# Seven products for ten instead of eight weight pairs in the second layer of a fused attention-plus-Mish block (Trainium2, one core)

## The chip, the cores and the metric

The kernel runs on one core of one Trainium2 chip. The metric is the device time of one execution in microseconds. An execution is timed as a whole; one more execution was profiled, and its record gives the start and the duration of every instruction on the engines: PE (TensorE, matmuls), PEld (its weight loads), DVE (VectorE), ACT (ScalarE), POOL (GpSimd) and SP (SyncE, which issues nearly all DMAs here). PSUM is the memory that PE writes and that DVE and ACT read.

## The reference

2048 tokens of 576 features, float32. One layer norm feeds two branches, and both are added to the input:

```python
xn = _layernorm(x)
q, k, v = split_heads(xn @ wqkv)            # 32 heads of 18
# each token attends to 8 tokens: itself and those 2, 4, ..., 14 before it
o = softmax_over_8(q . k * scale, mask) . v
A = o @ wo
h = xn @ w1 + b1                            # 4608 features (in reference: einsum)
B = (h * tanh(softplus(h))) @ w2            # Mish, then back to 576
return x + A + B
```

(The sketch keeps the arithmetic of the reference and shortens its code. In the reference the second branch is fed `xn`, too.)

## The kernel before, in words

**Precision.** Every matmul operand is kept as a high part (rounded to fp32r by an ACT cast) and a low part (the difference, taken by DVE or POOL). A product is three matmuls: high x high, high x low, low x high. So each weight tile and each activation costs a cast and a subtraction, on ACT and on DVE or POOL.

**Tiling.** The tokens are done in two halves (`hf` 0 and 1) of 1024, each in two blocks of 512 (`b`). The 4608 features of the hidden layer are 36 tiles of 128, taken as 18 pairs (`q`). In the second half the pairs come in the order 1, 2, ..., 17, 0 (`Q1`), but are still counted from 0.

**First layer** (`m1_part`, line 748). For one pair, 2 token blocks times 2 feature tiles are computed by seven products instead of eight, in six parts m0 to m5. PSUM banks are re-used inside a pair: `mish(hf, q, 1, 1, cur[3], cur["c22"])` at the end of m3 asks DVE (line 728) to add bank 3 and a copy `c22`, which ACT took from bank 1 at the end of m3 (line 717); m4 goes on accumulating in bank 3, so it must wait for this add. After the add come Mish (ACT, 729), the cast (ACT, 734) and the low part (POOL, 735).

**Second layer, the plain way** (`m2_pair` in the first half, `m2_cols` in the second, lines 783 and 896). A pair's activations times its two `w2` tiles: 4 chunks of 24 matmuls of 288 columns, with an eviction by DVE (lines 787, 899) for every six.

**Second layer by seven products** (second half only, for the first 2 x `OC` pairs, `p_item`, line 875). Two pairs together form a group `e`; token block x column half is a 2 x 2 scheme, done by seven items of 24 matmuls. It needs sums of weight quarters, T1 to T4, which the first half prepares when it meets a pair with 1 <= q <= 2 x `OC`: `t_sum` (line 304: T3 on DVE, T1, T2, T4 on POOL), `t_high` (ACT cast, 310), `t_low` (DVE, 315), `t_keep` (two DMAs to DRAM each). In the second half it needs sums of activations (`u_sum`, 817), casts (`u_high`, 823) and low parts (`u_low`, 829), and each item fetches its weights (`p_fetch`, 843). Pair q = 2 x `OC` of the second half is held raw and split by `a_split`.

**Attention.** The projections q, k, v (line 351, and `z_part`, 449, which does the last two groups of the second half by seven products with weight sums `z_...`) go to DRAM and come back as windows. A generator `attention(hf)` makes 73 steps for each half: eight head groups of nine steps. Of the nine, four multiply q by k (POOL, two instructions of line 542 each), one subtracts the maximum and calls the exponential, four multiply by v (POOL, two of line 580 each). The reduction of a product (DVE, 547 or 586) is held back and issued at the next step. After a group's last reduction, DVE transposes (606) and SP sends the result to DRAM (`o_send`, 615: four DMAs, eight for the last group).

**Output projection** (`wo_part`, line 1079): eight items of three parts at the end, by seven products too, on tiles `oa`, `ob`, `oS` that `o_split` makes (lines 927 to 958); their sources come by `o_load` (908), the sums of the first half by `y_load` (1054).

**The order of the work** is written out by hand. `plan` is a list of slots, each with one piece of PE work. A slot has a list `[1]` of things issued before its PE work (`before(i, fn)`) and a list `[0]` of its PE work and what is issued behind it. Inside a slot the order is: what the last slot left in `soon`, list `[1]` in the order in which it was filled, the Mish chains that the last slot left in `pend`, then list `[0]`. The engines keep this order:

```python
for fn in first + bg + (fns + held if i == at["m", 0, 1, 0] else held + fns):
```

For a pair of the first half, `spot(0, q, i)`, i = 0 to 9, are the slots m0, m1, chunk, m2, chunk, m3, chunk, m4, chunk, m5 (from q = 2 on); "slot 3 of pair 9" below means spot(0, 9, 3). Attention steps go to slots by a clock: every slot has a planned length, times a rate of its region (`marks`, `rate`), and a step falls due every 6.111 units, in the next allowed slot (in pairs from 1 on: slots 0, 3, 7 and 9). In the second half the slots of the steps are listed (`early`). `t_...` steps stand at slots 2 to 7 of a pair: T1 at 2, T2 at 3, T4 at 4, the cast of T3 and T1 at 4, the cast of T2 and T4 at 5. They are filled in ahead of the attention steps, so in one slot they come first.

## Time and profile before

| what | value |
|---|---|
| time, median of three | 1106.52 us (1106.3 to 1106.97) |
| time of the profiled execution | 1106.93 us |
| its span, first to last instruction | 1105.1 us |
| matmuls of `m2_pair` / `m2_cols` / `p_item` | 1728 / 960 / 672 |
| busy share: PE, DVE, ACT, POOL | 99%, 77%, 45%, 72% |

The 1.8 us between the span and the time lie around the program. A row of the timeline reads: start, duration, engine, line, operation, output tile <- input tiles, shape, count, and in brackets how long the engine stood idle before it and who ended that. Where several instructions are merged, the duration is that of all of them. A row of the windows reads: window, its length, then for PE, PEld, DVE, ACT and POOL the busy time and the number of instructions, the granted clock, the DMA share and GB/s.

### The profile page before, as it was taken

To read this page: it belongs to the slowest core of one execution; us is meant where nothing else is said; L and a number is where in the kernel's file an instruction comes from. 1 tells how busy PE (TensorE), PEld (TensorE's weight loads), DVE (VectorE), ACT (ScalarE), POOL (GpSimd) and SP (SyncE) were. 2 spreads that over 40 slices of the span, in tenths; PEclk is the share of its full clock that TensorE was granted. 3 is DMA by queue.
4 is the path that set the end of the run, shared out by engine and by line. 5 is a ranking of instruction groups with operands and counts; after the bars stand their busy time and mean duration, and the time that the engine had idled before them with its cause. 6 is when DMAs were issued, how large, how long until landed. Compare 5 with 4: busy or idle time off the path is not lost.

```text
span 1105.1 us, 18208 instructions
## 1 busy us (share of the span) xinstructions
PE 1098.0 (99%) x6550; PEld 1014.0 (92%) x6550; DVE 849.1 (77%) x1367; ACT 499.1 (45%) x917; POOL 790.8 (72%) x639
## 2 busy tenths in 40 slices
PE   8999999999999999999999999999999999999998
PEld 7999899999999999999999888989999999999998
DVE  6368788888889888888656567777886777777786
ACT  5544655544545543646333354434433344343353
POOL 2479777776769688685789568567698976867542
PEclk9999999999999999999999999999999999999999
DMA  6899696868777768676598799656674657776674
GB/s 200 286 311 313 231 335 244 283 234 263 254 269 242 272 225 293 234 265 219 171 316 277 237 348 327 228 192 209 222 225 171 211 196 224 244 293 216 181 232 140
DMA packets 178270, 271.60 MB, mean 246 GB/s; under 512 B 53218, under 2 KB 120068, under 8 KB 178180
## 3 DMA queue, kind: packets, MB, share of 16 engines
q1 hardware_dynamic: 178180, 270.44, 72.1%
q8 instruction: 52, 0.85, 0.3%
q14 instruction: 38, 0.31, 0.1%
HBM read 160.39 MB, written 110.00 MB: 245 GB/s over the span
## 4 chain that ended last, share of the span: by engine, by line
PE 92%; DMA 3%; DVE 2%; ACT 1%; SPq 1%; POOL 1%; issue 1%; DVEq 0%; POOLq 0%
PE h L683 28%; PE po L783 21%; PE po L896 11%; PE pq L351 11%; PE po L875 6%; PE h L689 5%; PE o L1079 5%; PE z L449 3%; DMA accP<-in_x 1%; DMA t<-kept_t 1%; DMA kv<-kv_d 1%; SPq L615 1%; DMA pw<-kept_T 0%; POOL act L735 0%; DMA acc<-in_x 0%
## 5 line engine op out<-in xcount | busy, mean ns | idle before, releaser
L783 PEld LDWEIGHTS po<-w,act 128*128 128x128 f32 x1728 | 236.3, 188 | 5.8 <-POOL act L735 0.4
L783 PE MATMUL po<-w,act 128*128 128x288 f32 x1728 | 240.6, 295 | 0.1
L542 POOL TENSOR_TENSOR pr<-q,kv 128x576 f32<-128x576 f32 x128 | 198.1, 1575 | 8.8 <-DMA q<-q_d 5.6
L735 POOL TENSOR_TENSOR act<-c,act 128x512 fp32r<-128x512 f32 x81 | 107.6, 1328 | 127.5 <-ACT act L734 126.1
L580 POOL TENSOR_TENSOR pv<-L,kv 128x576 f32<-128x576 f32 x128 | 177.9, 1488 | 26.1 <-DVE L L573 21.3
L787 DVE TENSOR_TENSOR acc<-po,acc 128x288 f32<-128x288 f32 x288 | 119.2, 448 | 29.2 <-PE po L783 28.3
L351 PE MATMUL pq<-wq,xt 128*128 128x432 f32 x672 | 136.2, 361 | 1.1 <-ACT xt L81 1.1
L896 PEld LDWEIGHTS po<-w,act 128*128 128x128 f32 x960 | 130.9, 188 | 2.8
L896 PE MATMUL po<-w,act 128*128 128x288 f32 x960 | 132.9, 295 | 0.0
L351 PEld LDWEIGHTS pq<-wq,xt 128*128 128x128 f32 x672 | 125.0, 188 | 7.8 <-ACT xt L81 1.6
L729 ACT ACTIVATE c<-c,b1c 128x512 f32<-128x512 f32 x81 | 58.7, 725 | 137.9 <-DVE c L728 137.6
L683 PE MATMUL h<-xt,t 128*128 128x512 f32 x432 | 110.5, 391 | 0.4 <-DVE rt L728 0.4
L683 PE MATMUL h<-S,t 128*128 128x512 f32 x432 | 110.4, 391 | 0.0
L586 DVE TENSOR_REDUCE og<-pv 128x144 f32<-128x1152 f32 x64 | 85.9, 1345 | 24.0 <-POOL pv L580 23.8
L683 PE MATMUL h<-xt,wa 128*128 128x512 f32 x432 | 103.9, 389 | 0.0
L717 ACT COPY c<-h 128x512 f32<-128x512 f32 x81 | 47.4, 585 | 123.1 <-PE h L689 72.0
L547 DVE TENSOR_REDUCE L<-pr 128x64 f32<-128x1152 f32 x64 | 85.8, 1342 | 21.8 <-POOL pr L542 21.7
L683 PEld LDWEIGHTS h<-xt,wa 128*128 128x128 f32 x432 | 81.0, 188 | 16.6
L875 PEld LDWEIGHTS po<-pw,u 128*128 128x128 f32 x672 | 91.9, 188 | 2.2
L875 PE MATMUL po<-pw,u 128*128 128x288 f32 x672 | 93.4, 294 | 0.0
L683 PEld LDWEIGHTS h<-xt,t 128*128 128x128 f32 x432 | 79.1, 188 | 15.3 <-DVE rt L728 0.9
L899 DVE TENSOR_TENSOR accP<-po,accP 128x288 f32<-128x288 f32 x160 | 68.9, 452 | 30.3 <-PE po L896 29.3
(228 smaller groups left out, 1851.4 us busy)
## 6 DMA issues: line engine op xcount, KB each, us to landing
kv<-kv_d SPq DMA_DIRECT2D x64, 396.0 KB, 5.0
kept_t<-t SPq DMA_DIRECT2D x36, 512.0 KB, 4.9
t<-kept_t SPq DMA_DIRECT2D x36, 512.0 KB, 6.6
rw<-in_w SPq DMA_DIRECT2D x36, 320.0 KB, 4.4
kept_wa<-wa SPq DMA_DIRECT2D x18, 640.0 KB, 4.6
kept_w<-w SPq DMA_DIRECT2D x20, 576.0 KB, 4.0
wa<-kept_wa SPq DMA_DIRECT2D x18, 640.0 KB, 5.3
w<-kept_w SPq DMA_DIRECT2D x20, 576.0 KB, 4.3
```

The source lines that it names most:

```text
L351: nc.tensor.matmul(pq[:, 0:432], XT[:, xi, tok], wt[wi][:, hl, 0:432], start=i == 0, stop=i == len(seq) - 1)
L542: nc.gpsimd.tensor_tensor(out=pr[:, x:x + hh], in0=q[:, j0 + x:j0 + x + hh, None, :].to_broadcast([P, hh, W, CU]), in1=win(kt, 0, CU, j0 + ...
L547: nc.vector.tensor_reduce(L[:, k, j0:j0 + hj].rearrange("p j w h -> p (j w h)"), pr.rearrange("p j w (h d) -> p (j w h) d", h=2), axis=AX, ...
L580: nc.gpsimd.tensor_tensor(out=pr[:, x:x + hj].rearrange("p j d w -> p j w d"), in0=L[:, k, x:x + hj, :, h:h + 1].to_broadcast([P, hj, W, DH]),
L586: nc.vector.tensor_reduce(og[:, c0:c0 + DH, :].rearrange("p d j -> p j d"), pr, axis=AX, op=ALU.add)
L683: nc.tensor.matmul(ph, wt[:, wl, wk * P:(wk + 1) * P], X[:, xs, :], start=first and i == 0, stop=last and i == len(seq) - 1, skip_group_ch ...
L735: nc.gpsimd.tensor_tensor(out=a[:, 1, :], in0=t, in1=a[:, 0, :].bitcast(F32), op=ALU.subtract)
L783: nc.tensor.matmul(po, acts[hf, q, b, j][:, al, tok], done["w2", hf, 2 * q + j][:, wl, c * HC:(c + 1) * HC], start=i == 0, stop=i == 5)
L787: nc.vector.tensor_tensor(out=t, in0=po, in1=t, op=ALU.add)
L875: nc.tensor.matmul(po, units[e, k, qq][:, al, tok], w[:, qq, wl, :], start=i == 0, stop=i == 5)
L896: nc.tensor.matmul(po, acts[hf, q, b, j][:, al, tok], done["w2", hf, 2 * q + j][:, wl, c * HC:(c + 1) * HC], start=i == 0, stop=i == 5)
L899: nc.vector.tensor_tensor(out=t, in0=po, in1=t, op=ALU.add)
```

## The change

`OC` goes from 4 to 5: five groups instead of four, so ten pairs of the second half are done by seven products. Everything that hangs on `OC` follows: pairs 9 and 10 of the first half now make T1 to T4, and pairs 8 and 9 of the second half (counted from 0) lose their `m2_cols` and are held raw for group 4. With it:

- Pair 10's block (1, 0) rests in slot `r3`.
- For q over 8, `t_low` stands behind the slot's PE work (list `[0]`). So do all the low parts of the `z` weights. The `z` weight work starts at slot 6 of pair 10, not slot 4 of pair 9, with both its rounds 28 slots apart.
- First half's attention: the rate from pair 16 on is 1.05 (it was 0.8), and one step instead of three lies in the second half's first pair. The steps up to pair 16 keep their slots.
- Second half's attention: `early` has three steps in pair 0 (it had one), one more in pair 5 and a longer list. Its last step lies one slot later, in the third instead of the second of the last four chunks.
- The preparation of `wo` starts at slot 0 of pair 13, not slot 3 of pair 11, with tighter spacing.

```diff
-OC = 4
+OC = 5
@@ raw_act
-...[b, j][q % {(1, 0): 4, (1, 1): 2}.get((b, j), 3)]
+...[b, j][3 if (q, b, j) == (2 * OC, 1, 0) else q % {(1, 0): 4, (1, 1): 2}.get((b, j), 3)]
@@ t steps of a pair
-            before(i + d, lambda f=f, name=name, q=q: f(q, name))
+            plan[i + d][f is not t_low or q <= 8].append(lambda f=f, name=name, q=q: f(q, name))
@@ z weights
-    i = spot(0, 9, 4)
+    i = spot(0, 10, 6)
-                d = 30 + 2 * n + (n >= 14) if k else 2 * n if n < 10 else (19, 20, 22, 23, 25, 26, 27)[n - 10]
-                before(i + d, lambda f=f, name=name, k=k: f(name, k))
+                d = 28 * k + (2 * n if n < 10 else (19, 20, 22, 23, 25, 26, 27)[n - 10])
+                plan[i + d][kind != "o"].append(lambda f=f, name=name, k=k: f(name, k))
@@ attention steps
-    behind_next.add(at["m", 1, 10, 3])
+    behind_next.add(at["m", 1, 2 * OC + 2, 3])
-    marks = [..., spot(0, 1, 0), spot(0, 2 * OC + 1, 0), at["q", 1, 0, 0, 0],
+    marks = [..., spot(0, 1, 0), spot(0, 9, 0), spot(0, 16, 0), at["q", 1, 0, 0, 0],
-    rate = (1.15, 0.4, 0.5, 0.8, 1.15, 1.25, 0)
+    rate = (1.15, 0.4, 0.5, 0.8, 1.05, 1.15, 1.25, 0)
-    last_steps = [spot(1, 0, i) for i in (0, 2, 4)]
+    last_steps = [spot(1, 0, 0)]
-    early = {0: (8,), 1: (0, 2, 4, 6, 8), 2: (0, 4, 7), 3: (0, 3, 6), 4: (0, 4, 7), 5: (0, 3, 7), 6: (1, 4, 7),
-             7: (0, 4, 7), 8: (1, 4, 8), 9: (1, 3, 7)}
+    early = {0: (2, 4, 8), 1: (0, 2, 4, 6, 8), 2: (0, 4, 7), 3: (0, 3, 6), 4: (0, 4, 7), 5: (0, 3, 6, 8),
+             6: (1, 4, 7), 7: (0, 3, 7), 8: (1, 4, 7), 9: (0, 4, 7), 10: (1, 4, 8), 11: (1, 3, 7)}
@@ wo weights
-    i = spot(1, *(11,3))
+    i = spot(1, 13, 0)
-        k = i + 10 + (2, 5, 10, 15, 20, 25, 30, 35, 40)[n]
+        k = i + 10 + (2, 5, 8, 12, 15, 19, 23, 27, 31)[n]
```

More of the change, by code (lines that the diff above doesn't have):

```diff
@@ L703, in raw_act @@
         tag, n = {(0, 0): (("raw", 0), ("raw", 1), ("raw", 2)), (1, 0): (("mn", 2), ("mn", 3), ("mn", 0), ("r3", 0)),
-                  (0, 1): (("raw", 3), ("mn", 4), ("mn", 1)), (1, 1): (("tt", 0), ("tt", 1))}[b, j][q % {(1, 0): 4, (1, 1): 2}.get((b, j), 3)]
+                  (0, 1): (("raw", 3), ("mn", 4), ("mn", 1)), (1, 1): (("tt", 0), ("tt", 1))}[b, j][3 if (q, b, j) == (2 * OC, 1, 0) else q % {(1, 0): 4, (1, 1): 2}.get((b, j), 3)]
         if (tag, n) not in rslot:
@@ L1507, in block_kernel @@
             ok[spot(0, q, i)] = i in (0, 3, 7, 9) and (q > 1 or i)
-    marks = [at["q", 0, 2, 0, 1], at["q", 0, 3, 0, 0], spot(0, 1, 0), spot(0, 2 * OC + 1, 0), at["q", 1, 0, 0, 0],
+    marks = [at["q", 0, 2, 0, 1], at["q", 0, 3, 0, 0], spot(0, 1, 0), spot(0, 9, 0), spot(0, 16, 0), at["q", 1, 0, 0, 0],
              at["z", 0, 0], spot(1, 0, 0)]
-    rate = (1.15, 0.4, 0.5, 0.8, 1.15, 1.25, 0)
+    rate = (1.15, 0.4, 0.5, 0.8, 1.05, 1.15, 1.25, 0)
     T = [0.0]
```

## The prediction

> **What bounds the kernel now.** I read the page first, then the chain of waits, then the timeline engine by engine around the places that the diff touches.

> ```profile
> PE 1098.0 (99%) x6550; PEld 1014.0 (92%) x6550; DVE 849.1 (77%) x1367; ACT 499.1 (45%) x917; POOL 790.8 (72%) x639
> PEclk9999999999999999999999999999999999999999
> PE 92%; DMA 3%; DVE 2%; ACT 1%; SPq 1%; POOL 1%; issue 1%; DVEq 0%; POOLq 0%
> ```

> PE is busy nearly all the time at a high granted clock, and the chain that ended last is PE for 92%. So a matmul less is time less, and a wait that reaches PE is time more; the other engines count only where they reach PE. They are not far from it. These are pairs 9 and 10 of the first half, which the change loads:

> ```profile
> 308.60:332.60 24.00, 24.00 (x148) 22.02 (x147) 21.14 (x32) 10.82 (x20) 19.77 (x18) 1.00 0.70 238
> 332.60:356.70 24.10, 24.10 (x148) 22.11 (x147) 22.18 (x31) 11.26 (x20) 22.11 (x17) 1.00 0.78 257
> ```

> In pair 10, DVE and POOL are both busy for 22.1 of 24.1 us, and PE for all of it.

> **The matmuls removed.** Two pairs by the plain way are 8 chunks, by seven products 7 items.

> ```profile
> 699.28 3.17 PE po L875 x24
> 846.71 3.18 PE po L896 x24
> ```

> 8 x 3.18 - 7 x 3.17 = 3.25 us; I take **-3.2**. No row speaks against it, since PE is not waiting in either stretch.

> **The second half's other work for group 4.** Per group the seven products need 14 casts and 14 low parts for 8 of each before, and 8 sums of activations, with four evictions fewer. Of the 14 low parts 6 fall to DVE, of the sums 6. Nearest rows:

> ```profile
> L829 DVE TENSOR_TENSOR u<-rm,u 128x512 fp32r<-128x512 f32 x12 | 13.5, 1125 | 6.2 <-ACT u L823 6.2
> L817 DVE TENSOR_TENSOR rm<-ra,rm 128x512 f32<-128x512 f32 x6 | 6.9, 1155 | 0.9 <-ACT rm L729 0.9
> 759.00:784.00 25.00, 25.00 (x151) 22.82 (x151) 20.01 (x34) 12.55 (x19) 10.84 (x9) 1.00 0.56 198
> 784.00:805.00 21.00, 21.00 (x129) 19.29 (x128) 17.61 (x26) 9.08 (x16) 17.98 (x14) 1.00 0.60 216
> 687.68 1.63 PE L683 MATMUL h<-xt,t 128*128 128x512 f32 x6 [0.42 <-DVE rt L728]
> ```

> So DVE gains 12 x 1.14 - 4 x 0.45 = 11.9 us over two pairs. The last group of before (the two windows) already carries this, with DVE at 37.6 of 46 us and PE without a gap. I counted the steps through the list `early`: group 4's slots are those of group 3 of before, two pairs later, and its steps are nine later, so each slot holds the same kind of step. I cost it at **0**, hidden behind PE; between 0 and the largest PE wait that this half shows behind DVE, the 0.42 us of the last row. At the start of the second half, attention begins two or three steps earlier; that row's wait may go or stay. I take **-0.3**, bounds -0.5 and +0.5. The three fetches and the kept sums more are DMA work in windows at 0.56 to 0.78 of the DMA engines, with several microseconds between issue and use: 0.

> **Pairs 9 and 10 of the first half.** Each gets four weight sums, two casts and two low parts.

> ```profile
> L304 POOL TENSOR_TENSOR twT<-rw,twT 128x288 f32<-128x288 f32 x16 | 15.4, 963 | 1.3
> L304 POOL TENSOR_TENSOR twT<-rw 128x288 f32<-128x288 f32 x8 | 10.4, 1299 | 0.0
> L304 DVE TENSOR_TENSOR twT<-rw,rw 128x288 f32<-128x288 f32 x8 | 9.3, 1157 | 0.0
> L315 DVE TENSOR_TENSOR twT<-twT,twhT 128x576 fp32r<-128x576 f32 x16 | 13.8, 894 | 0.2
> L310 ACT CAST twhT<-twT 128x576 fp32r<-128x576 f32 x16 | 10.8, 676 | 16.4 <-POOL twT L304 16.2
> ```

> That is 2 x 0.96 + 1.30 = 3.2 us for POOL and 1.16 + 2 x 0.89 = 2.9 us for DVE in each pair. POOL gives back one `z` sum in pair 9 and two in pair 10, so both engines stay just inside 24 us. The sum of the work fits; the order is what does not. Look at the ACT row: it stood idle 16.2 us in all, waiting for POOL's sums, and ACT runs its instructions in program order. Behind that cast stands the copy `c22` of m3, behind the copy DVE's add, and m4 needs the add. Pair 7 of before shows the whole chain, on POOL, ACT, DVE, PE:

> ```profile
> 271.73 1.89 POOL L304 TENSOR_TENSOR twT<-rw,twT 128x288 f32<-128x288 f32 x2
> 273.66 0.67 ACT L310 CAST twhT<-twT 128x576 fp32r<-128x576 f32 x1 [1.29 <-POOL twT L304]
> 274.24 0.58 ACT L717 COPY c<-h 128x512 f32<-128x512 f32 x1
> 275.04 0.68 DVE L728 TENSOR_TENSOR c<-h,c 128x512 f32<-128x512 f32 x1
> 276.66 1.53 PE L683 MATMUL h<-xt,t 128*128 128x512 f32 x6
> ```

> T4 ends at 273.62, the cast at 274.33, the copy at 274.82, the add at 275.72; m4 starts at 276.66. So add = T4 + 2.1, and the slack is 0.9 us. That m4 waits for this add where it is late, the row at 687.68 has shown: m4 of a pair, 0.42 us behind DVE line 728.

> In pairs 2 to 8 no attention step lies in slot 3. In pairs 9 and 10 one does, in both kernels (the clock of the steps is unchanged up to pair 16), and there T2 comes ahead of the step and T4 behind it. POOL and PE in pairs 9 and 10 of before:

> ```profile
> 317.12 1.30 POOL L735 TENSOR_TENSOR act<-c,act 128x512 fp32r<-128x512 f32 x1
> 318.37 2.99 POOL L580 TENSOR_TENSOR pv<-L,kv 128x576 f32<-128x576 f32 x2
> 324.64 1.30 POOL L735 TENSOR_TENSOR act<-c,act 128x512 fp32r<-128x512 f32 x1 [3.28 <-ACT act L734]
> 324.82 1.53 PE L683 MATMUL h<-xt,t 128*128 128x512 f32 x6
> 325.89 2.54 POOL L580 TENSOR_TENSOR pv<-L,kv 128x576 f32<-128x576 f32 x2
> 332.17 3.52 POOL L580 TENSOR_TENSOR pv<-L,kv 128x576 f32<-128x576 f32 x2
> 340.67 1.29 POOL L735 TENSOR_TENSOR act<-c,act 128x512 fp32r<-128x512 f32 x1
> 343.01 3.28 POOL L542 TENSOR_TENSOR pr<-q,kv 128x576 f32<-128x576 f32 x2
> 348.90 1.53 PE L683 MATMUL h<-xt,t 128*128 128x512 f32 x6
> ```

> *Pair 9.* POOL comes to T1 at 318.42. T1, T2, the step's two products, T4: 1.30 + 0.95 + 2.95 + 0.95 = 6.15, so T4 ends at 324.6 and the add at 326.7. m4 is due at 324.82: **+1.8**. A step's two products last between 2.54 and 3.52 us in these rows, so the bounds are 1.4 and 2.4.

> *Pair 10.* POOL comes to T1 at 341.96; 2.25 + 3.25 + 0.95 gives 348.4, the add 350.5, m4 due at 348.90: +1.6. But pair 9 also leaves a lag. In before the add stood 2.4 us ahead of m4, and after it DVE has evictions, statistics, a reduction and a weight's low part before the next add:

> ```profile
> 322.46 0.69 DVE L728 TENSOR_TENSOR c<-h,c 128x512 f32<-128x512 f32 x1 [0.80 <-ACT c L717]
> 328.74 0.68 DVE L728 TENSOR_TENSOR c<-h,c 128x512 f32<-128x512 f32 x1
> ```

> In before these two are 6.3 us apart with little idle time between. Now the first ends as m4 starts, so the second, its Mish and POOL's low part come 1.7 us later against PE, and POOL then runs without a gap to T1 of pair 10. Full carry gives 3.3, none 1.6; I take **+2.9**, since POOL's rows in pair 10 leave no room to catch up. The low parts that now stand behind their slots no longer delay the add; that is worth at most the 0.2 us between copy and add in pair 7, which I leave in the 2.1.

> [...]

> **The end.** The second half's last step moves one chunk (3.2 us) later, nearer to the output projection. DVE, PE and SP there:

> ```profile
> 1039.05 1.36 DVE L586 TENSOR_REDUCE og<-pv 128x144 f32<-128x1152 f32 x1 [0.57 <-POOL pv L580]
> 1042.44 0.77 DVE L606 STREAM_TRANSPOSE oT<-og 128x576 f32<-128x576 f32 x1
> 1048.66 0.43 DVE L955 TENSOR_TENSOR ob<-ot,ob 64x256 fp32r<-64x256 f32 x1
> 1049.15 0.53 PE L1079 MATMUL o<-wo_r,ob 128*128 128x288 f32 x2
> 1043.24 4.28 SPq L615 DMA_DIRECT2D o_d<-oT  x8
> ```

> DVE's last reduction comes where the transpose stands now, the transpose a chunk later, both still ahead of line 955, for which PE's second product waits until 1049.15 already. From 1039.05 to 1049.1 DVE is idle for only 0.65 us (behind ACT), so one reduction more in it moves line 955, and PE, by its 1.35 us: **+1.3**, bounds 0.3 and 2.8. The upper one holds what SP adds: its eight sends of 4.3 us now stand ahead of the loads for the next item at about 1048 rather than 1043.

> **Slots elsewhere.** The `z` weights and `wo` rest move inside stretches where DVE is at 17 to 21 of 24 us: 0. The rate of 1.05 brings about two steps (3 us of DVE, 6 us of POOL) into pairs 16 and 17, where POOL is at 11.9 of 24 us in the last: 0.

> **The sum.** -3.2 + 0 - 0.3 + 1.8 + 2.9 + 1.3 = +2.5 us. On the profiled 1106.93 (span 1105.1 and 1.8 around it) this gives 1109.4, and on the median of 1106.52, 0.4 lower, **1109.0 us**, 0.23% slower. What a measurement of this kernel can tell from no change is about 0.2%, 2.2 us: below 1104.3 is faster, above 1108.7 slower.

> **The rivals.**

> *The chain of T4 doesn't reach PE* (the other side). The mechanism is the same cast on ACT; it decides by when T4 ends, 15.1 us after m0 of the pair (17.3 to m4 less 2.1). If POOL gets there, as in pair 7 at 14.2, both waits are gone: -3.2 - 0.3 + 0.5 at the end = 1103.5. For it: no PE wait shows anywhere in the first half beyond pair 1. Against: the step in slot 3 alone is 3.0 us, against 0.9 of slack. Chance 0.18.

> *One short wait, no lag.* DVE catches up in pair 9, since its low part of `w2` moves from the pair's end to its middle, and the end absorbs half: -3.2 - 0.3 + 1.5 + 1.2 + 0.6 = 1106.3. For it: DVE has 1 to 2 us of idle time per pair. Chance 0.32.

> *The waits grow.* [...] Chance 0.12.

> **How the numbers follow.** My forecast has 0.38. Its spread is about 1 us, so a third of it lies under 1108.7. Slower: 0.25 + 0.12 and the upper part of the second rival's spread, 0.08: 0.45. Faster: 0.18 and a little of the second rival's lower part, 0.02: 0.20. Same: 0.35. The range runs from the first rival's time to just under the third's: 1103.4 to 1111.0, with half of the first rival below it and half of the third above.

> **What would show it.** PE's m4 in pairs 9 and 10 should stand idle behind DVE line 728, with ACT line 310 just ahead waiting for POOL line 304, and T4 ending over 15.1 us after m0; no such idle time means the first rival. A wait in pair 10 no longer than in pair 9 means that no lag was carried. At the end, PE's wait for `ob` of line 955 should grow by about 1.3 us. In group 4, PE should show no gap. If PE's idle time adds up as forecast but the time doesn't, the 3.2 us of matmuls are what I have wrong.

## The result, and the profile after

| | before | after |
|---|---|---|
| time, median of five | 1106.88 us (1106.3 to 1106.99) | 1136.38 us (1134.79 to 1137.64) |
| ratio, 95% interval | | 1.0267 (1.0256 to 1.0279) |
| profiled execution, span | 1106.93, 1105.1 us | 1137.47, 1135.7 us |
| matmuls | 6550 | 6526 |

The change is 29.5 us slower. I forecast 1109.0 us in a range of 1103.4 to 1111.0: the sign was right, the size was not near. These are the busy time and the chain's engines of the page after:

```profile
PE 1105.2 (97%) x6526; PEld 1015.5 (89%) x6526; DVE 860.1 (76%) x1381; ACT 504.3 (44%) x927; POOL 804.3 (71%) x647
PE 36%; POOL 4%; DVE 4%; issue 1%; ACT 1%; DMA 1%; SPq 0%; POOLq 0%; DVEq 0%; ACTq 0%
```

These shares don't compare with the 92% of before: the shares of after add up to 47%, since its chain can be followed back only to 612.65 us, and of the part that is followed PE is about three quarters. What the page does show is that work of the others grew by 2% at most while PE's own share of the span fell from 99% to 97%. So it isn't that an engine became the bound; PE has to wait for them at particular places. PE's timeline of after names the places:

```profile
327.31 1.66 PE L683 MATMUL h<-xt,t 128*128 128x512 f32 x6 [2.18 <-DVE c L728]
...
353.76 2.82 PE L683 MATMUL h<-xt,t 128*128 128x512 f32 x6 [2.08 <-DVE c L728]
...
469.19 3.45 PE L783 MATMUL po<-w,act 128*128 128x288 f32 x24 [1.31 <-DVE acc L787]
...
540.31 3.46 PE L783 MATMUL po<-w,act 128*128 128x288 f32 x24 [1.12 <-DVE acc L787]
...
606.80 1.45 PE L449 MATMUL z<-z_T,S 128*128 128x432 f32 x3 [4.19 <-ACT zqs L458]
...
667.39 2.49 PE L683 MATMUL h<-xt,t 128*128 128x512 f32 x6 [3.85 <-DVE rt L728]
...
759.09 3.17 PE L875 MATMUL po<-pw,u 128*128 128x288 f32 x22 [0.84 <-DVE u L829]
...
1050.10 1.67 PE L683 MATMUL h<-xt,t 128*128 128x512 f32 x6 [1.74 <-DVE c L728]
...
1075.88 0.53 PE L1079 MATMUL o<-wo_r,ob 128*128 128x288 f32 x2 [0.97 <-DVE ob L955]
...
1087.38 1.45 PE L1079 MATMUL o<-wo,oS 128*128 128x288 f32 x6 [1.79 <-DVE y L1083]
```

The idle time in brackets isn't all. Look at the first two rows: the same six matmuls, after nearly the same idle time, took 1.66 and 2.82 us. After some of the waits PE runs at half its pace for a while. The windows behind these two waits show it in the granted clock, 1.00 and 0.50 (the third number from the end of each row):

```profile
327.31:330.72 3.41, 3.41 (x20) 3.07 (x21) 3.38 (x9) 1.85 (x3) 1.97 (x2) 1.00 0.98 329
353.90:357.31 3.41, 3.41 (x9) 2.65 (x10) 3.41 (x7) 1.70 (x3) 2.12 (x2) 0.50 0.87 281
```

So I counted PE's **loss**: for every matmul the distance to the next one's start, less the undisturbed distance that the same pair of shapes keeps in the kernel before (the mean of those within 30 ns of their median). All losses of a trace add up to 10.2 us before and 43.9 after. The difference of 33.7, less 3.1 for the matmuls that are gone, is the 30.6 us between the spans.

| place | loss before | loss after |
|---|---|---|
| start of the kernel | 5.9 | 6.1 |
| m4 of pairs 9 and 10, first half | 0 | 2.4 + 3.9 |
| a chunk in pair 15, one in pair 16 | 0 | 1.6 + 1.1 |
| last chunks of the first half, transposes | 0 | 1.4 + 0.6 |
| `z` part, at 602 and 618 us | 0 | 6.0 + 1.1 |
| second half, m4 of pair 1 | 0 | 5.7 |
| m4 of pair 2 | 0.7 | 0 |
| pairs 5 and 6 | 0 | 3.6 |
| m4 of pair 17 | 0 | 2.0 |
| output projection | 0.5 | 5.4 |
| all other matmuls | 3.1 | 3.0 |

Three of these places show how one wait passes through several queues. In the `z` part, POOL and ACT after, then POOL and ACT before:

```profile
593.43 2.66 POOL L633 TENSOR_TENSOR s<-s,xt 128x512 f32<-128x512 f32 x2
596.05 6.54 POOL L542 TENSOR_TENSOR pr<-q,kv 128x576 f32<-128x576 f32 x4
602.56 1.71 POOL L633 TENSOR_TENSOR s<-xt,s 128x512 f32<-128x512 f32 x1
604.35 1.27 POOL L633 TENSOR_TENSOR s<-s,xt 128x512 f32<-128x512 f32 x1
...
605.65 0.62 ACT L665 CAST S<-s 128x512 fp32r<-128x512 f32 x1 [6.51 <-POOL s L633]
606.18 0.39 ACT L458 COPY zkv<-z 128x288 f32<-128x288 f32 x1
606.47 0.28 ACT L458 COPY zqs<-z 128x144 f32<-128x144 f32 x1
```

```profile
582.27 3.40 POOL L580 TENSOR_TENSOR pv<-L,kv 128x576 f32<-128x576 f32 x2
585.53 1.29 POOL L633 TENSOR_TENSOR s<-xt,s 128x512 f32<-128x512 f32 x1
586.90 1.30 POOL L633 TENSOR_TENSOR s<-s,xt 128x512 f32<-128x512 f32 x1
...
588.23 0.62 ACT L665 CAST S<-s 128x512 fp32r<-128x512 f32 x1 [0.25 <-POOL s L633]
```

Before, one attention step (two products) stands between two of POOL's sums of activations; after, two steps do (four products, 6.5 us). ACT's cast of the sum waits 6.51 us for them. Behind the cast stand the copies that empty PE's bank, and PE waits 4.19 us for the copies.

At m4 of pair 1 of the second half, ACT, POOL and DVE of after:

```profile
660.80 0.42 ACT L567 ACTIVATE L<-L 128x256 f32<-128x256 f32 x1
...
662.75 4.90 POOL L580 TENSOR_TENSOR pv<-L,kv 128x576 f32<-128x576 f32 x4 [10.07 <-ACT rt L717]
...
665.38 1.35 DVE L586 TENSOR_REDUCE og<-pv 128x144 f32<-128x1152 f32 x1 [2.26 <-POOL pv L580]
666.66 0.68 DVE L728 TENSOR_TENSOR rt<-h,rt 128x512 f32<-128x512 f32 x1
```

DVE's add for m4 stands behind a reduction that waits for POOL's products, which wait for the exponential and DVE's division. The releaser that the POOL row names is an ACT copy; of the things that the products need, DVE's division (line 573), done at 662.5, is the one that fits. Before, this slot held another kind of step.

At the end, DVE, SP and ACT of after:

```profile
1072.84 0.77 DVE L606 STREAM_TRANSPOSE oT<-og 128x576 f32<-128x576 f32 x1
...
1073.63 4.19 SPq L615 DMA_DIRECT2D o_d<-oT  x8
1077.92 0.45 SPq L1054 DMA_DIRECT2D y<-y_d  x1
...
1082.94 1.02 DVE L1083 TENSOR_TENSOR y<-o,y 128x288 f32<-128x288 f32 x2 [0.24 <-DMA y<-y_d]
...
1083.16 2.15 SPq L908 DMA_DIRECT2D o<-o_d  x2
...
1085.70 0.38 ACT L927 COPY ot<-o 128x256 f32<-128x256 f32 x1 [3.29 <-DMA o<-o_d]
```

The transpose comes 0.3 us ahead of the first matmul of the output projection (1073.16); before, it came 4.9 us ahead (1042.44, 1047.37). SP's sends stand ahead of its loads of `y` and `o`; ACT waits 3.29 us for the load, DVE's eviction stands behind that, and PE at 1087.38 waits 1.79 us for the eviction.

### The profile page after: what moved, and what is told of

Its sections match the earlier page's. It is cut to its first block, busy times and chain, and to the rows that moved or that the text cites. A ratio compares the mean times of both kernels' runs of the same rounds, so it can differ in the third digit from the quotient of the medians.

```text
span 1135.7 us, 18213 instructions
## 1 busy us (share of the span) xinstructions
PE 1105.2 (97%) x6526; PEld 1015.5 (89%) x6526; DVE 860.1 (76%) x1381; ACT 504.3 (44%) x927; POOL 804.3 (71%) x647
## 5 line engine op out<-in xcount | busy, mean ns | idle before, releaser
L783 PEld LDWEIGHTS po<-w,act 128*128 128x128 f32 x1728 | 236.4, 188 | 10.0 <-DVE acc L787 4.3
L783 PE MATMUL po<-w,act 128*128 128x288 f32 x1728 | 241.2, 295 | 3.4 <-DVE acc L787 3.3
L542 POOL TENSOR_TENSOR pr<-q,kv 128x576 f32<-128x576 f32 x128 | 200.1, 1592 | 16.6 <-DVE og L586 9.9
L580 POOL TENSOR_TENSOR pv<-L,kv 128x576 f32<-128x576 f32 x128 | 177.4, 1482 | 34.4 <-ACT rt L717 10.1
L735 POOL TENSOR_TENSOR act<-c,act 128x512 fp32r<-128x512 f32 x75 | 101.5, 1353 | 116.8 <-ACT act L734 109.4
L683 PE MATMUL h<-xt,t 128*128 128x512 f32 x432 | 112.9, 397 | 9.9 <-DVE c L728 6.0
L875 PEld LDWEIGHTS po<-pw,u 128*128 128x128 f32 x840 | 114.8, 188 | 6.0 <-DVE accP L881 1.4
L875 PE MATMUL po<-pw,u 128*128 128x288 f32 x840 | 117.2, 295 | 2.5 <-DVE accP L881 1.0
L729 ACT ACTIVATE c<-c,b1c 128x512 f32<-128x512 f32 x75 | 54.4, 725 | 137.9 <-DVE c L728 137.7
L683 PE MATMUL h<-S,t 128*128 128x512 f32 x432 | 110.4, 391 | 0.0
L896 PEld LDWEIGHTS po<-w,act 128*128 128x128 f32 x768 | 104.6, 188 | 2.6 <-DVE accP L899 0.3
L896 PE MATMUL po<-w,act 128*128 128x288 f32 x768 | 106.5, 295 | 0.0
L586 DVE TENSOR_REDUCE og<-pv 128x144 f32<-128x1152 f32 x64 | 85.9, 1344 | 25.8 <-POOL pv L580 25.7
L683 PE MATMUL h<-xt,wa 128*128 128x512 f32 x432 | 103.9, 389 | 0.0
L683 PEld LDWEIGHTS h<-xt,t 128*128 128x128 f32 x432 | 80.1, 190 | 25.9 <-DVE c L728 6.7
L683 PEld LDWEIGHTS h<-xt,wa 128*128 128x128 f32 x432 | 80.9, 188 | 16.6
L683 PEld LDWEIGHTS h<-S,t 128*128 128x128 f32 x432 | 77.9, 188 | 13.2 <-ACT rm L717 0.5
L717 ACT COPY c<-h 128x512 f32<-128x512 f32 x75 | 43.9, 585 | 92.2 <-PE h L689 54.7
```

The lines of the kernel that those rows point to most:

```text
L542: nc.gpsimd.tensor_tensor(out=pr[:, x:x + hh], in0=q[:, j0 + x:j0 + x + hh, None, :].to_broadcast([P, hh, W, CU]), in1=win(kt, 0, CU, j0 + ...
L580: nc.gpsimd.tensor_tensor(out=pr[:, x:x + hj].rearrange("p j d w -> p j w d"), in0=L[:, k, x:x + hj, :, h:h + 1].to_broadcast([P, hj, W, DH]),
L586: nc.vector.tensor_reduce(og[:, c0:c0 + DH, :].rearrange("p d j -> p j d"), pr, axis=AX, op=ALU.add)
L683: nc.tensor.matmul(ph, wt[:, wl, wk * P:(wk + 1) * P], X[:, xs, :], start=first and i == 0, stop=last and i == len(seq) - 1, skip_group_ch ...
L729: nc.scalar.activation(t, ph if fresh else t, AF.Mish, bias=b1c[:, f:f + 1])
L735: nc.gpsimd.tensor_tensor(out=a[:, 1, :], in0=t, in1=a[:, 0, :].bitcast(F32), op=ALU.subtract)
```

## The experiments

**My theory after the result:** each loss belongs to one place where a step was moved in the hand-written order, and it goes when that order is put back. **The rival:** the fifth group's extra work leaves DVE and POOL no room; then the losses come back elsewhere, whatever the order.

**1. T4 ahead of the step** (the changed kernel, pairs 9 and 10).

```diff
-   (0,0,1,2,2,3,4,3,4,5)
+   (0,0,1,1 if q > 8 else 2,2,3,4,3,4,5)
```

> The changed kernel with T4 of pairs 9 and 10 issued one slot earlier, ahead of the attention step of slot 3. Theory (order on POOL, not load): T4 ends about 3 us earlier in both pairs, so PE's waits for DVE line 728 at m4 of pair 9 (2.18 us) and pair 10 (2.08 us), and the slowed matmuls behind the second, are gone: 1136.4 - 6.3 = 1130.1 us, at most 1131.5. Rival (load: four sums, two casts and two low parts do not fit beside the attention): the step's products come 0.9 us later, DVE waits for them instead, and PE waits somewhere else in pairs 9 to 11: 1134.5 or more.

Measured: 1133.45 us, ratio 1.0227 (1.0209 to 1.0245). Both waits are gone; pair 11 now loses 0.9. That is 5.4 us less loss, as the theory has it, but its time fell by only 2.9: in the profiled execution other waits lost more (pair 1 of the second half 6.5, not 5.7), chiefly with more slow matmuls behind them (at pair 1 the clock is at half for 6.83 us, in the changed kernel for 3.41, after the same wait). The price was measured again in run 10.

**2. The first half's attention clock put back** (the changed kernel).

```diff
-spot(0, 9, 0), spot(0, 16, 0), at["q", 1, 0, 0, 0],
+spot(0, 9, 0), at["q", 1, 0, 0, 0],
-rate = (1.15, 0.4, 0.5, 0.8, 1.05, 1.15, 1.25, 0)
+rate = (1.15, 0.4, 0.5, 0.8, 1.15, 1.25, 0)
-last_steps = [spot(1, 0, 0)]
+last_steps = [spot(1, 0, i) for i in (0, 2, 4)]
```

> The changed kernel with the first half's attention clock of the kernel before (no 1.05 from pair 16 on, three last steps in slots 0, 2 and 4 of the second half's first pair). Theory: the steps of the first half met the z part and the last chunks in a new order; with the old one PE's waits at about 539 (1.4 us), 602 to 609 (6.0) and 618 us (1.1) are gone: 1136.4 - 8.5 = 1127.9. The wait of 3.85 us in pair 1 of the second half (and its slow matmuls, 5.7 in all) should stay, or grow by up to 3, since two steps of the first half now share slots with the first steps of the second. Rival (the waits belong to the load of the ten sums and of the z weights): they stay, 1135 or more.

Measured: 1131.72 us, ratio 1.0224 (1.0208 to 1.0239). The losses in the last chunks and in the `z` part are gone (9.1 to under 1). In their place one of 3.6 us has come at 642 us, where steps of both halves share slots 2 and 4 of the second half's first pair.

**3. Low parts of the `z` weights ahead of their slots** (the changed kernel).

```diff
-plan[i + d][kind != "o"].append(...)
+before(i + d, ...)
```

> The changed kernel with the low parts of the z weights ahead of their slots' PE work again (list 1), nothing else. Theory: the low part that DVE takes just ahead of line 787 in pairs 15 and 16 is what makes PE wait 1.31 and 0.83 us there: 1136.4 - 2.5 = 1133.9. Rival: those waits come of the steps of the attention that stand between, DVE works the same list one place earlier, and the time stays within 1 us of 1136.4.

Measured: 1136.14 us, ratio 1.0256 (1.0237 to 1.0274). The loss in pair 15 fell from 1.6 to 0.5, but 1.0 came at the next m4; pair 16's 1.1 is gone. So of 2.7 us 1.5 are left. The time is the rival's all the same: in the profiled execution more slow matmuls stand behind other waits (m4 of pair 17 loses 3.6, not 2.0; pair 1 of the second half 6.5, not 5.7).

**4. The kernel before with the first half's new clock alone** (the edit of run 2 the other way round, OC stays 4).

> The kernel before (four groups) with one part of the change alone: the first half's attention clock (1.05 from pair 16 on, one last step in the second half's first pair). Theory: the waits at the last chunks of the first half and in the z part come of this edit alone, whatever OC is: 1106.9 + 1.4 + 6.0 + 1.1 = 1115.4, with PE waiting about 4 us for ACT behind POOL in the z part. Rival: they need the later z weights or the fifth group's load: within 1 us of 1106.9.

Measured: 1116.01 us, ratio 1.0082 (1.0066 to 1.0099). POOL, PE and ACT in the `z` part:

```profile
586.95 6.55 POOL L542 TENSOR_TENSOR pr<-q,kv 128x576 f32<-128x576 f32 x4
...
597.70 1.45 PE L449 MATMUL z<-z_T,S 128*128 128x432 f32 x3 [4.18 <-ACT zqs L458]
...
596.55 0.62 ACT L665 CAST S<-s 128x512 fp32r<-128x512 f32 x1 [6.51 <-POOL s L633]
```

These are the rows of the changed kernel to 0.01 us, in a kernel with four groups. This edit alone costs 9 us; the fifth group has no part in it.

**5. The kernel before with two steps more in the second half's first pair**.

```diff
-early = {0: (8,), ...
+early = {0: (2, 4, 8), ...
```

> The kernel before (four groups) with one part of the change alone: two more attention steps in the second half's first pair, slots 2 and 4, so every later step of the half stands two places earlier in the list. Theory (the order of step and slot decides): m4 of pair 1 waits about 4 us for DVE line 728, behind a reduction of line 586, and its first matmuls run slow: +5.7; pairs 2 to 9 hold steps that they didn't hold before and may add 0 to 4; the end comes two chunks earlier, 0 to -0.5: 1112 to 1116.5 us. Rival (the wait in pair 1 needs the changed first half or the fifth group): under 1108.

Measured: 1118.28 us, ratio 1.0101 (1.0086 to 1.0116). DVE and PE at m4 of pair 1:

```profile
650.45 1.35 DVE L586 TENSOR_REDUCE og<-pv 128x144 f32<-128x1152 f32 x1 [2.26 <-POOL pv L580]
651.72 0.68 DVE L728 TENSOR_TENSOR rt<-h,rt 128x512 f32<-128x512 f32 x1
...
652.45 2.25 PE L683 MATMUL h<-xt,t 128*128 128x512 f32 x6 [3.85 <-DVE rt L728]
```

Again the same waits, 2.26 and 3.85 us, with four groups; the loss is 5.7. The time is above what I expected, since another 3.7 is lost at 633 us, where both halves' steps share slots, and 1.3 in pair 5.

**6. One step more in pair 11** (the changed kernel), so that pairs 12 to 17 hold what they held before.

```diff
-10: (1, 4, 8), 11: (1, 3, 7)}
+10: (1, 4, 8), 11: (1, 3, 7, 9)}
```

> The changed kernel with one attention step more in pair 11 of the second half (slot 9), so that pairs 12 to 17 hold the same steps in the same slots as the kernel before, and the last step lies in the second of the last four chunks again. Theory (order): PE's wait of 1.74 us in pair 17 (2.0 in all) and those at the output projection (1.5 + 0.4 + 3.6, less the 0.5 of the kernel before) are gone: 1136.4 - 7.0 = 1129.4. Rival A (only the last step's place counts, not the order in pair 17): 1131.4. Rival B (the end is late because of the later wo weights and the load of the fifth group): 1135 or more.

Measured: 1133.09 us, ratio 1.0233 (1.0216 to 1.025). SP and PE at the output projection:

```profile
1069.53 4.19 SPq L615 DMA_DIRECT2D o_d<-oT  x8
...
1075.43 0.53 PE L1079 MATMUL o<-wo_r,ob 128*128 128x288 f32 x2
```

The output projection loses 0.5 us, as in the kernel before, and m4 of pair 17 nothing: both hang on the place of the last steps. The step put into pair 11 costs 1.9 at 918 us. A new loss of 1.1 has come at a chunk of pair 17; it stays in runs 7 to 10, and no run shows its cause (DVE takes a low part of `wo`, line 980, shortly before it, which in the kernel before it does not). The time fell by 3.3, not by 7.

**7. All orders mended together** (five groups): T4 as in run 1, the clock of run 2, and this list.

```diff
-early = {0: (2, 4, 8), ..., 5: (0, 3, 6, 8), 6: (1, 4, 7), 7: (0, 3, 7), 8: (1, 4, 7), 9: (0, 4, 7), 10: (1, 4, 8), 11: (1, 3, 7)}
+early = {0: (8,), ..., 5: (0, 3, 7), 6: (1, 4, 7), 7: (0, 4, 7), 8: (0, 4, 7), 9: (0, 3, 6), 10: (1, 4, 8),
+         11: (1, 3, 5, 7, 9), 12: (1, 3, 4, 5, 7, 9), 13: (1, 3, 4, 5, 7, 9)}
```

> The changed kernel (five groups, ten pairs) with the orders mended together: T4 of pairs 9 and 10 ahead of the step; the first half's clock as in the kernel before; in the second half one step in pair 0 as before, and the missing steps put behind the last group (two in pair 11, one each in pairs 12 and 13), so that pairs 14 to 17 hold what they held before. Theory (order): 5.4 (pairs 9 and 10) + 8.5 (first half's last steps) + 5.7 (pair 1) + 3.5 (pairs 5 and 6) + 2.0 (pair 17) + 4.9 (end) = 30.0 less than 1136.4: 1106.4 us; with up to 4 us for the steps squeezed into pairs 11 to 13 up to 1110.4. Rival (load: the fifth group's sums, casts and low parts do not fit, and the waits come back elsewhere): 1118 or more.

Measured: 1118.25 us, ratio 1.0095 (1.008 to 1.0111). All losses that it was to remove are gone, 18.1 us of the time. New ones came: 5.0 at 884 us (pair 11), 2.2 in pairs 12 and 13, 1.1 at 1032, and 1.9 more than in run 1 in pair 11 of the first half. Both theories hold in part: the order decides where the steps stand, but the four steps have no free place. The list loses four places because pairs 10 and 11 now hold three steps each, for five before.

**8. SP's order, and other slots.** Run 7 with the `z` weights two slots later (rounds 26 apart), and slot 8 for slot 4 in pairs 12 and 13.

```diff
-i = spot(0, 10, 6)
+i = spot(0, 10, 8)
-d = 28 * k + ...
+d = 26 * k + ...
-12: (1, 3, 4, 5, 7, 9), 13: (1, 3, 4, 5, 7, 9)}
+12: (1, 3, 5, 7, 8, 9), 13: (1, 3, 5, 7, 8, 9)}
```

> As the last kernel (five groups, orders mended), with two places changed. The z weights start two slots later (slot 8 of pair 10, rounds 26 apart), so that SP issues the w1 loads of pair 12 ahead of the three z loads; and the steps squeezed into pairs 12 and 13 stand in slot 8 (behind m4) and no longer in slot 4 (ahead of m4). Theory (order): in the last kernel the first matmuls of pair 11's m3 and m4 waited 1.0 and 1.25 us since SP issued the w1 load about 8 us later, behind a z load that waits for a tile; that goes, -2.0 to -2.7. The wait at m4 of pair 12 and its slow matmuls (5.0) and the two behind it (0.4 + 1.8) fall to 3 or less: -4. The waits of pairs 15 and 16 (1.6 + 1.1) stay. 1118.3 - 6.5 = 1111.8 us. Rival (load): pairs 12 and 13 wait as long at another line, and the time is 1116 or more. For less than the kernel before, 1107, all waits over 0.5 us would have to go, which neither theory gives.

Measured: 1119.85 us, ratio 1.0118 (1.0101 to 1.0135). SP of run 7, then of this run:

```profile
350.62 4.96 SPq L388 DMA_DIRECT2D zB<-in_wq  x3
355.63 0.42 SPq L276 DMA_DIRECT2D kept_t<-t  x1
356.11 1.32 SPq L199 DMA_DIRECT2D rw<-in_w  x2
```

```profile
351.77 1.99 SPq L199 DMA_DIRECT2D rw<-in_w  x2
...
357.10 1.98 SPq L388 DMA_DIRECT2D zB<-in_wq  x3
```

The `w1` load of the next pair no longer stands behind the `z` loads, and pair 11's loss (2.8) is gone. The rest fell out otherwise than I expected: the 5.0 of pair 11 in the second half (which the expectation wrongly puts in pair 12) stayed, and slot 8 cost more than slot 4, 6.2 for 2.2.

**9 and 10. The missing steps spread, and T4 late again beside it.** Run 8 with other places; run 10 leaves T4 where the change puts it.

```diff
-11: (1, 3, 5, 7, 9), 12: (1, 3, 5, 7, 8, 9), 13: (1, 3, 5, 7, 8, 9)}
+11: (1, 3, 7, 9), 12: (1, 3, 4, 5, 7, 9), 13: (1, 3, 4, 5, 7, 9), 14: (1, 3, 4, 5, 7, 9)}
```

> As the last kernel, with the four missing steps at other places: one in slot 9 of pair 11 (not slots 5 and 9), and one in slot 4 of each of the pairs 12, 13 and 14. Theory: the wait of 3.17 us at m4 of pair 11 (5.0 with its slow matmuls) came of the step in slot 5, whose products POOL takes between the additions of line 884; it goes (-5.0). Slot 4 cost 0.4 and 1.8 in pairs 12 and 13 against 6.2 for slot 8 in the last kernel; with a third step 2.2 to 4. 1119.9 - 5.0 - 6.2 + 2.2 to 4 = 1111 to 1113 us. Rival (POOL and DVE have no room for four steps more behind the last group, wherever they stand): 1116 or more.

> The same with T4 of pairs 9 and 10 behind the attention step again, as the changed kernel has it: the price of this order alone in a kernel whose other orders are mended. Theory: the two waits of about 2.2 us are there, and 0 to 3 us of slow matmuls behind them: 4.4 to 7.4 us more than the kernel beside it. Rival (the waits are absorbed, since DVE works off its lag in pair 11): under 2 us more.

Measured: 1116.84 us, ratio 1.0087 (1.0072 to 1.0102), and 1121.61 us, ratio 1.0135 (1.0119 to 1.0152). Run 9 is the fastest with five groups, and still 9.7 us behind the kernel before. Slot 5 of pair 11 was the cause of its 5.0, which is gone; but pair 12 now loses 5.9, and another 2.6 are lost at 960 us. Run 10 is 4.8 slower than run 9 (3.8 between the profiled executions). m4 of pair 9 in run 9, then in run 10:

```profile
324.40 1.53 PE L683 MATMUL h<-xt,t 128*128 128x512 f32 x6
```

```profile
326.80 2.89 PE L683 MATMUL h<-xt,t 128*128 128x512 f32 x6 [2.17 <-DVE c L728]
329.48 1.00 PE L689 MATMUL h<-xt,wa 128*128 128x512 f32 x2
```

Pair 9's loss is 4.0 here with the slow matmuls, and pair 10 doesn't wait at all. So it is in all five traces in which slow matmuls follow the wait of pair 9 (runs 2, 6, 10, 11 and 12); in the two without them (the changed kernel and run 3) pair 10 waits. That the other engines catch up while PE runs slowly is my reading of it.

**11. Three steps in pair 5** (the changed kernel).

```diff
-5: (0, 3, 6, 8), ..., 11: (1, 3, 7)}
+5: (0, 3, 7), ..., 11: (1, 3, 7, 9)}
```

> The changed kernel with three attention steps in pair 5 of the second half, as in the kernel before (slots 0, 3, 7 for 0, 3, 6, 8), and the fourth in slot 9 of pair 11, so that only pairs 6 to 11 hold other steps. Theory (the extra step): of PE's waits in pairs 5 and 6 (1.1 + 1.0 + 1.2 us) the last two go and the first stays, as in the kernel before with two steps early (1.1 at one place): 1136.4 - 2.2 = 1134.2; the end is as in the changed kernel. Rival (the sums and low parts of the groups themselves): all three stay. What pairs 6 to 11 add with their new order is open: 0 to 3 us.

Measured: 1142.68 us, ratio 1.0319 (1.0302 to 1.0336). In pair 6 both waits are gone and pair 5's stays, as the theory has it. But pairs 6 to 11 hold other steps now, and the fifth group loses 3.9. PE there:

```profile
866.33 4.32 PE L875 MATMUL po<-pw,u 128*128 128x288 f32 x19 [0.57 <-POOL u L829]
```

Without this edit PE has no gap in that stretch. Another 3.5 are lost at 927 us, at the chunk of pair 11 where run 6, with the same step in slot 9, lost 1.9. A group's sums and low parts fit beside one order of steps and not beside another.

**12. The second round of the `z` weights two slots earlier** (the changed kernel; 26 for 28).

> The changed kernel with the second round of the z weights 26 slots behind the first, not 28 (two slots earlier), nothing else. Theory (the z weights' place makes PE wait in pairs 15 and 16): the wait of 1.6 us at pair 15 (in all) shrinks or goes, since the low part of line 405 that DVE took just ahead of lines 728 and 787 there now falls two slots earlier, and that of pair 16 (1.1) too, since DVE then comes to it without lag: up to -2.7, 1133.7 us. Rival (DVE and POOL are full there, wherever the weights stand): both waits stay at 1.1 to 1.6, and the time within 1 us of 1136.4.

Measured: 1135.17 us, ratio 1.0258 (1.0241 to 1.0275). The chunk in pair 15 doesn't wait, but the next m4 loses 1.2, since DVE's low part of a `z` weight now stands 3.59 us idle behind POOL ahead of that add; pair 16 keeps 1.1. Here the loss moves; run 3 took part of it away. What would free DVE in pairs 15 and 16 stays open.

## Why the forecast's size was wrong, point by point

- **The matmuls, -3.2: right.** Spans and losses give -3.1. Pairs 9 and 10 alone lost more than this, so the forecast's sign was not luck.
- **Pairs 9 and 10, +1.8 and +2.9: the mechanism was right, the size too small.** POOL, ACT and DVE of after, pair 9:

```profile
321.38 3.31 POOL L580 TENSOR_TENSOR pv<-L,kv 128x576 f32<-128x576 f32 x2
324.54 0.81 POOL L304 TENSOR_TENSOR twT<-rw,twT 128x288 f32<-128x288 f32 x1
...
325.38 0.67 ACT L310 CAST twhT<-twT 128x576 fp32r<-128x576 f32 x1 [4.14 <-POOL twT L304]
325.96 0.58 ACT L717 COPY c<-h 128x512 f32<-128x512 f32 x1
...
326.57 0.69 DVE L728 TENSOR_TENSOR c<-h,c 128x512 f32<-128x512 f32 x1 [3.06 <-ACT c L717]
```

  T4, cast, copy, add, m4, in the order that was forecast. T4 ended 0.75 us later, since POOL came to T1 0.84 later (319.26); from there its four pieces took 6.1 us, as forecast. DVE's low part beside the products (line 315 at 321.76) took 1.74 us, the next one (328.63) 0.75. The loss is 6.3, not 4.7. Pair 10 waited no longer than pair 9, so the lag that I added wasn't carried; slow matmuls took its place. Run 10 measured 4.8 for this order alone, with a loss of 4.0 in pair 9 and none in pair 10.
- **The second half's other work, 0: right for group 4 only.** PE has no gap from 785 to 1040 us. But I checked the kind of step slot by slot for group 4 alone. Pairs 1 to 6 hold steps shifted by two or three in the list. Pairs 5 and 6 lose 3.6, and in run 11, without the extra step in pair 5, 2.2 of that were gone. The same edit shifts the steps of pair 6 by one, so whether the number of steps or their order did it isn't shown.
- **The start of the second half, -0.3, bounds -0.5 and +0.5: this step failed.** I argued from the one wait that I could see (0.7 in pair 2, which did go) and not from what each slot would hold. The wait that came is 5.7 at m4 of pair 1; run 5 showed that two steps more in the first pair bring it without any fifth group.
- **Slots elsewhere, 0: this step failed most, by 11.8.** I looked at the rate of 1.05 where it begins, in pairs 16 and 17, and not at what it does to all steps after them: every one falls into another slot, and in the `z` part two come between two sums. Run 4 showed 9 us of that from this edit alone. Pairs 15 and 16 are the other 2.7. That the place of the `z` weights bears on them is shown by run 3, which left 1.5, and run 12, which moved one; neither brought the time down by more than 1.2, and the cause as a whole stays open.
- **The end, +1.3, bounds 0.3 and 2.8: the first wait was right** (1.0 idle, 1.5 lost, 1.0 more than before). The second, over SP's sends, cost 3.9 with its slow matmuls, and m4 of pair 17 another 2.0 that I hadn't looked for. Run 6 took both away with the last step's place.
- **The rivals:** the third, that the waits grow, named the kind of outcome. Its time, just above the range's upper end of 1111.0, rests on a cost that no run shows: the changed kernel took 1136.38 us, and in its trace four waits of PE, of 1.79 to 4.19 us, were each followed by 3.41 us at half the clock. The first is refuted: the chain of T4 does reach PE. The second was right that no lag is carried, but it counted on one short wait and 1106.3 us; both pairs waited over 2 us.

So the forecast worked through the places where work was added and costed the places where steps were only moved at nothing. The moved steps cost most, counted by losses: first half's clock 9 us (run 4), second half's start 5.7 (run 5), the end and pair 17 some 7 (run 6), against 6.3 for the added weight sums. In time, with what came elsewhere, run 6 gained 3.3, and the order of the weight sums was worth 2.9 (run 1) and 4.8 (run 10). Whether an order exists in which the fifth group pays stays open. Five groups without any new wait would give 1106.9 - 3.1 = 1103.8 us; no version here came nearer than 1116.8.

## What to carry to other kernels

Where four in-order queues are interleaved by hand, a step that moves by one slot is a new order for everything behind it: list what each slot holds before and after the edit, in all stages that the shift reaches, and not only where work is added. A product, a reduction or a load queued ahead of the one small instruction that frees PE's bank costs PE time, however idle that instruction's engine is on average: in the `z` part PE stood idle for 4.19 us behind copies of ACT, which is busy for 44% of the span. And check that the places a change takes away (four slots for steps here) exist elsewhere, before counting what it saves.

## What the runs showed of the hardware

I hadn't expected that waits of about 2 us would slow PE down afterwards. In the fourteen traces (before, after and twelve experiments) I compared each loss of a single matmul start over 0.8 us (past the first 30 us) with the distances in the 4 us behind it:

| PE starts late by | cases | followed by slow matmuls |
|---|---|---|
| 0.8 to 1.5 us | 78 | 0 |
| 1.5 to 2.7 us | 29 | 16, each losing 1.1 to 1.7 us more |
| 3.3 to 4.4 us | 19 | 19, each losing 1.3 to 1.8 us more |

(The same wait of several runs counts as several cases.) m4 of pair 9 starts 2.3 us late in the changed kernel and in run 3 without slow matmuls, and in runs 2, 6, 10, 11 and 12 with them.

0.52 of a window is about 1.8 us. All 19 waits of 3.3 to 4.4 us were followed by 1.3 to 1.8 us of further loss, and 16 of the 29 waits of 1.5 to 2.7 us by 1.1 to 1.7 us. For another version of this kernel my estimate from these counts is some 1.5 us more behind a wait of over 3 us, and the same in about half of the cases behind one of 1.5 to 2.7 us.
